# First two token blocks multiplied in plain float32: operands undivided, the norm's g moved into the weight conversion, schedule positions set anew

## The chip, the cores and the metric

The kernel runs on one core of one Trainium2 chip. The metric is device microseconds of one execution. Engines are named as in the profile: PE (TensorE matmul; PEld is its weight load), DVE (VectorE), ACT (ScalarE), POOL (GpSimd), SP (the engine whose queue issues nearly all DMAs).

## The reference, cut to what matters

Eight heads of a linear attention are normalised row by row, laid side by side as a 4608 x 512 matrix x, and sent through a two-layer network with a softplus between the layers.

```python
q, k, v: (8, 8, 576, 64) float32          # batch, heads, tokens, head_dim
w_in: (512, 2048), w_out: (2048, 512)     # come out of numpy as float64
kv  = np.einsum('bhsd,bhse->bhde', k, v)
out = np.einsum('bhsd,bhde->bhse', q, kv)
rms = np.sqrt(np.mean(out * out, axis=-1, keepdims=True) + 1e-06)
x   = (out / rms * g_norm).astype(np.float32)    # then (B,H,S,D) -> (B*S, H*D)
h   = x @ w_in
g   = np.maximum(h, 0.0) + np.log1p(np.exp(-np.abs(h)))
return (g @ w_out).astype(np.float32)
```

## The kernel before

**Divided operands.** The two large multiplications run in fp32r, a matmul form that keeps fewer bits than float32. To keep the accuracy, each operand is divided into three fp32r parts, and each product is three fp32r matmuls that accumulate in one PSUM bank. A part is made by a copy that rounds (ACT, `high`), a subtraction (DVE, `low`) and a multiply-add (DVE, `less`). Weights need one ACT operation more (`low_up`, line 514) and end with `third` (ACT). Of the first eight weight tiles the step `less` is done by two matmuls with the identity (`less_by_pe`, lines 525 and 526) in place of DVE.

**Tiles and steps.** Tokens are cut into 36 tiles of 128 and into 12 blocks of three tiles (384 tokens); d_ff = 2048 is cut into 16 chunks of 128. The first phase works on one block and one chunk per `step(s)`: four chunks for each of blocks 0 to 3 and six for each of blocks 4 to 11, 64 steps in all. A step is `mm1` (12 matmuls of 128x384, line 864), softplus on ACT (line 886), the division of its result g into three parts (ACT line 888, DVE lines 875 and 879), and `mm2` for each of the three tiles (3 matmuls of 128x512 each, line 871, so nine a step). Phases 1 and 2 do the remaining chunks on blocks of 512 tokens with a seven-product scheme (`wide_step`, products on line 1066, second layer on line 1137); partial sums go through DRAM.

**What comes ahead of a step.** For a tile of x: k and v of its batch are loaded and multiplied (`kv_of`, line 696), the result is copied by ACT (line 704), q is loaded and transposed (PE line 776, later DVE line 751), the rows are q times kv (`out_rows`, line 720), ACT squares them (line 793), DVE sums (line 724), POOL takes the root (lines 727 and 728), DVE multiplies (`norm`, line 732), and PE transposes the tile (line 738). For the six tiles of blocks 0 and 1 the transposed tile is then divided from PSUM (`split`: ACT line 640, DVE lines 643 and 646) and also copied to DRAM for the later phases (ACT line 802, SP line 803). Later tiles are loaded from DRAM again (`x_again`, line 841) and then divided.

**Weights.** A weight tile (128 x 512) arrives as float64, 512 KB (line 423). Six DVE operations (lines 438, 442, 447, 455, 460, 464) and two ACT operations (lines 434, 451) turn it into float32. The factor g_norm of the norm is put into w_in when it is divided: ACT line 501 with the scale `g_down`, DVE line 508 with `g_col`.

**Order.** All work is recorded as tasks with an engine, a guessed duration, a position `pos` and the buffers taken and given back. A planner in the kernel (`Plan.order`) sorts the tasks by position and readiness; the instructions are then issued in that fixed order, each engine in its own queue. The lists P0 to P7 are the hand-set positions. Where the planner sees PE free before the seventh step it puts in matmuls of the identity (`warm`, line 1232) that compute nothing; the profile shows 52. Buffers are rings of slots; some slots (`heirs`) come free only when an older ring's slots on the same memory are done. The chunk loads of k and v use a ring of four slots (`e`).

Of the kernel before, what the change touches and what calls it, by code (L numbers as in the profile page):

```python
# [18 lines left out]
P = 128  # L19
# [3 lines left out]
DOWN_G = 1.0 - 0.99 * 2.0 ** -13  # L23
E = 1.0 / RADIX

# [181 lines left out]
def kernel(  # L207
# [47 lines left out]
    P0 = [-45.94, -26.77, -11.8, 0.28, -29.91, -5.64, -2.86, 3.84, -103.4, -98.98, -69.3, -76.66, -68.5, -24.67, -23.22, -34.97, 8.15, -43.02, 7.47, 9.69, 7.18, 18.16, -12.1, 4.75, 1.0, 106.19, 31.3, 6.28, 7.19, 5.22]  # L255
    P4 = [-30.17, -6.08, 16.93, -33.9, -22.35, -28.91, -17.33, -7.12, -18.68, -2.69, 0.62, 2.73, -7.38, -1.86, 1.1, 1.72, 5.22, -13.65, 3.22, 0.88, 43.88, 43.95, -0.17, -0.32, 44.8, 40.82, -20.17, -6.56, 6.41, 10.03, -10.73, 0.23, 2.8, 0.42, -9.48, -5.03]
    P5 = [1.24, -5.69, -2.28, -3.57, 1.72, 0.53, 6.68, -5.83, 3.01, -2.95, 3.35, 1.4, -6.96, 0.27, -5.34, -2.29]
    P6 = [1.05, 6.24, 4.29, 4.08, -1.52, -2.85, 1.21, -0.34, 3.11, 3.1, -1.07, -0.73, -0.88, 9.99, 5.7, 5.69, 0.13, 0.46]
    P7 = [-23.78, -17.98, -11.85, -14.93, 0.41, 1.61, 7.35, 2.7, -25.02, -6.6, -15.2, -4.48, -2.14, 0.64, 2.93, 0.97, 4.67, 5.36, 3.33, 6.57, -10.37, 2.36, -14.11, -9.89, -7.11, 12.91, -2.89, 14.55, 12.59, 9.35]
    CONVERT, FETCH, EARLY, LATER = P0[:8], P0[8:16], P0[16:27], P0[27:]  # L260
    P1 = [49.11, 48.77, 51.0, 80.9, 122.61, 131.29, 2.87, 53.84, 71.21, 480.08, 304.47, 150.69]
    P2 = [24.08, 35.56, 23.68, 37.26, 50.08, 83.13, 74.26, 112.0, 102.25, 108.09, 139.38, -110.13, 88.34, 208.35, 423.47, -209.77, 170.15, -245.78, 423.49, 179.94, -7.53]
    P3 = [2.14, 2.48, 6.41, -16.53, 0.86, 2.79, 4.01, -16.44, 3.79, 3.96, 2.19, 1.79, 0.72, 1.35, 1.55, -1.03]
# [3 lines left out]
    EARLIER = P3[15]  # L267
    PACE = 2.5
    BY_PE = 12
    AT_ONCE = 2 * TB  # L270
# [11 lines left out]
    g_down = const.tile([P, 1], F32, name="g_down")  # L282
# [24 lines left out]
    pieces = sb.tile([P, 12, PIECE], F32R, name="pieces")  # L307
    for i in range(3):
# [4 lines left out]
    minus_r = space("gv1", 4 * WIDE, False, F32R)[:, 3 * NT:3 * NT + P]  # L313
# [5 lines left out]
                 h=2, o=2, tp=1, s0=1, s1=1, s2=1, s3=1, w=15, wh=3, u=4, u1=1, gvp=2, xl=2, ab=2)  # L319
# [7 lines left out]
    heirs.update({("w", 12 + i): [("n", 3 * i + j) for j in range(3)] for i in range(3)})  # L327
    plan = Plan(rings, heirs)
    slot, add = plan.slot, plan.add

    def new(s, shape, dtype=F32):
# [17 lines left out]
        elif r == "w":  # L349
            s.tile = shaped(pieces[:, i] if i < 12 else space(f"w{i}", PIECE, True, F32R), shape, dtype)  # L350
        elif r == "n":
            s.tile = shaped(space(f"w{12 + i // 3}", PIECE, False)[:, i % 3 * d_model:], shape, dtype)
        elif r == "wh":
# [46 lines left out]
    factors_done = {}  # L400
# [13 lines left out]
    def weight(j, pos, fetch_pos, behind):  # L414

        c, of_out = divmod(j, 2)
        raw, w = slot("rawb" if j % 2 and c < 8 else "raw"), slot("m")
# [9 lines left out]
        if wide:  # L427
# [30 lines left out]
            def rest():  # L458
                pf = p.tile.bitcast(F32)
                nc.vector.scalar_tensor_tensor(out=pf, in0=words_of()[0], scalar=2.0 ** -52, in1=pf,  # L460
                                               op0=ALU.mult, op1=ALU.mult)

            def total():
                nc.vector.tensor_tensor(out=new(w, [P, d_model]), in0=t.tile.bitcast(F32),
                                        in1=p.tile.bitcast(F32), op=ALU.add)
# [9 lines left out]
        else:  # L475
            ready = add("DVE", 450, lambda: nc.vector.tensor_copy(new(w, [P, d_model]), raw.tile[:, :, 0]),
                        [f], pos, [w], [raw])
        if c < OWN:
            divide(j, w, ready, pos, c < 4)
# [4 lines left out]
    def divide(j, w, ready, pos, by_pe=False):  # L484

        c, of_out = divmod(j, 2)
        dst = slot("w")
        w_slots[of_out, c] = dst
        factors_done[of_out, c] = split_weight(w, lambda x: x, d_model, dst, [ready], pos, not of_out, by_pe)

    def split_weight(w, part_of, n, dst, ready, pos, of_in, by_pe=False):

        d = slot("m")

        def src():
            return part_of(w.tile)

        def high():
            x = new(dst, [P, 3, n], F32R)[:, 0]
            if of_in:  # L500
                nc.scalar.activation(x, src(), func=AF.Identity, scale=g_down)
            else:
                nc.scalar.activation(x, src(), func=AF.Copy, scale=DOWN)

        def low():
            hi = dst.tile.bitcast(F32)[:, 0]
            if of_in:
                nc.vector.scalar_tensor_tensor(out=new(d, [P, n]), in0=src(), scalar=g_col, in1=hi,
                                               op0=ALU.mult, op1=ALU.subtract)
            else:  # L510
                nc.vector.tensor_tensor(out=new(d, [P, n]), in0=src(), in1=hi, op=ALU.subtract)

        def low_up():
            nc.scalar.activation(dst.tile[:, 1], d.tile, func=AF.Copy, scale=RADIX)

        def less():
            nc.vector.scalar_tensor_tensor(out=d.tile, in0=d.tile, scalar=-RADIX, in1=dst.tile.bitcast(F32)[:, 0],
                                           op0=ALU.mult, op1=ALU.add)

        def third():  # L520
            nc.scalar.activation(dst.tile[:, 2], d.tile, func=AF.Copy, scale=-E / (1.0 + E))

        def less_by_pe():
            y = new(bank, [P, n])
            nc.tensor.matmul(y, lhsT=ident_r, rhs=dst.tile[:, 0], start=True, stop=False)
            nc.tensor.matmul(y, lhsT=minus_r, rhs=dst.tile[:, 1], start=False, stop=True)

        def third_of_bank():
            nc.scalar.activation(dst.tile[:, 2], bank.tile, func=AF.Copy, scale=-E / (1.0 + E))

        more = 0 if n == d_model else -210
        a = add("ACT", (710 if of_in else 640) + more, high, ready, pos, [dst])
        b = add("DVE", (750 if of_in else 700) + more * 1.25, low, [a], pos, [d], [w])
        if by_pe:
            bank = slot("h")
            e = add("ACT", 640, low_up, [b], pos, [], [d])
            b2 = add("PE", 500, less_by_pe, [e], pos, [bank])
            e2 = add("ACT", 600, third_of_bank, [b2], pos, [], [bank])
            return [a, e, e2]
        e = add("ACT", 640 + more, low_up, [b], pos)  # L540
        b2 = add("DVE", 700 + more * 1.25, less, [b, e], pos)
        e2 = add("ACT", 640 + more, third, [b2], pos, [], [d])
        return [a, e, e2]

# [8 lines left out]
    def both(p, fetch, pos):  # L553
# [16 lines left out]
        def rest():  # L570
# [9 lines left out]
                         split_weight(w0, lambda x: x, d_model, forms[p][0], [l0], pos, True),  # L580
                         split_weight(sa, lambda x: x, d_model, forms[p][1], [d2], pos + 0.1, True),
                         split_weight(sb_, lambda x: x, d_model, forms[p][2], [d4], pos + 0.2, True),
                         split_weight(w1, lambda x: x[:, q4:], q4, forms[p][3], [l1], pos + 0.3, True)]
        for c in (2 * p, 2 * p + 1):
            if c >= OWN:
                w, ld = load_weight(2 * c + 1, fetch + 0.4)
                divide(2 * c + 1, w, ld, pos + 1.4)

    forms, forms_done, w_there = {}, {}, {}
# [38 lines left out]
    def split(t, x, ready, pos):  # L628
        n, i = divmod(t, TB)
        if i == 0:  # L630
            xv_slots[n] = slot("xv")
# [6 lines left out]

        def high():
            nc.scalar.activation(cols(0, F32R), x.tile, func=AF.Copy, scale=DOWN)  # L640

        def low():
            nc.vector.tensor_tensor(out=cols(1, F32R), in0=x.tile, in1=cols(0), op=ALU.subtract)  # L643

        def less():
            nc.vector.scalar_tensor_tensor(out=cols(2, F32R), in0=cols(1), scalar=-RADIX, in1=cols(0),
# [20 lines left out]
    def kv_of(b):  # L667
# [7 lines left out]
        for p in range(NP + 1):  # L675
            tail = p == NP
            ks, vs = (slot(f"tail{i}" if tail else "e") for i in range(2))
# [29 lines left out]
    def rows(t):  # L707
# [90 lines left out]
        if t < BY_PE:  # L798
            a = add("PE", 440, turn_x, [a], pos + 0.5, [xp], [x])
            if t < AT_ONCE:  # L800
                split(t, xp, a, pos + 0.5)
            a = add("ACT", 600, lambda: nc.scalar.copy(new(xg, [P, KD, P]), xp.tile), [a], pos + 1, [xg], [xp])
# [46 lines left out]
    def step(s):  # L849
        n, c = ORDER[s]  # L850
        cs = CHUNKS[n]
        h, g, gv = slot("h"), slot("g"), slot("gv")
# [4 lines left out]
        kept = c >= 4  # L857

# [15 lines left out]
        def low():  # L874
            nc.vector.tensor_tensor(out=gv.tile[:, 1], in0=g.tile, in1=gv.tile.bitcast(F32)[:, 0], op=ALU.subtract)

        def less():
            f32 = gv.tile.bitcast(F32)
            nc.vector.scalar_tensor_tensor(out=gv.tile[:, 2], in0=f32[:, 1], scalar=-RADIX, in1=f32[:, 0],
# [6 lines left out]
        a = add("ACT", 490, lambda: nc.scalar.activation(new(g, [P, NT]), h.tile, func=AF.Softplus, scale=1.0 + E),  # L886
# [13 lines left out]
    sums, mm2s = [], {}  # L900

# [11 lines left out]
    def leave(ph, t, bank, done, pos):  # L913

        ot = slot("m")
        if ph == LAST and t == n_tiles - 1:
# [15 lines left out]
            new(ot, [P, d_model]), bank.tile, func=AF.Copy, scale=scale if ph == LAST else 1.0),  # L932
# [335 lines left out]
```

## Time and profile before

Three runs took 857.61, 857.70 and 859.12 us (median 857.7). The profiled execution has a span of 856.4 us from its first to its last instruction, 1.3 us less than the median.

| engine | busy us | share | instructions |
|---|---|---|---|
| PE | 843.0 | 98% | 6464 |
| PEld | 754.1 | 88% | 6464 |
| DVE | 704.1 | 82% | 995 |
| ACT | 520.6 | 61% | 980 |
| POOL | 76.6 | 9% | 79 |

| event of the start | us from the span's start |
|---|---|
| first DVE operation on a weight (line 438) | 4.73 |
| last chunk of batch 0's k issued, landed | 12.59, 18.49 |
| first multiplication by the norm (line 732) | 25.69 |
| first `mm1` (line 864) begins | 44.09 |
| first `mm2` (line 871) begins | 58.26 |
| sixth `mm1` begins | 78.84 |

A busy PE is not always PE at work: its matmuls are shown with their whole passage, and the fillers on line 1232 count as busy. How the work stands is read from the start times in the chain of waits and in the timeline. The granted clock is full in all 40 slices of the page. The DMA engines' mean share is 1.08 between 4.0 and 26.5 us (315 GB/s) and 0.94 between 26.5 and 79 us (244 GB/s).

### The profile page before, as it was taken

Reading aid. Unit: us, or ns where it says so; the run is one execution under the profiler, and the core shown is the slowest. Engines: PE = TensorE matmul, PEld = TensorE weight load, DVE = VectorE, ACT = ScalarE, POOL = GpSimd, SP = SyncE. Lnnn points to the kernel's source line nnn. Section 1 sums busy time; section 2 is a strip of 40 time slices with the busy share of each in tenths; the row PEclk is TensorE's granted clock in tenths of the full one; section 3 lists DMA queues with packets and bytes.
Section 4 is the critical chain, followed back from the end, with each engine's and each line's share of the span. In section 5 each row is a group of like instructions: output and inputs, shape, how many; then the busy total and the mean of one; then the engine's idle time right before and its main releaser. Section 6 shows DMA issues by size and latency. Waiting matters only on the chain.

```text
span 856.4 us, 17075 instructions
## 1 busy us (share of the span) xinstructions
PE 843.0 (98%) x6464; PEld 754.1 (88%) x6464; DVE 704.1 (82%) x995; ACT 520.6 (61%) x980; POOL 76.6 (9%) x79
## 2 busy tenths in 40 slices
PE   8899999999999999999999999999999999999998
PEld 5578898999898999999999999998999899999996
DVE  7888898888788889798898788878788766788873
ACT  6766665446344567766667665655868555566654
POOL 0351223111113300000000000000000000000000
PEclk9999999999999999999999999999999999999999
DMA  9998997778884755436644546645364753777864
GB/s 283 297 233 212 261 273 232 185 245 218 214 188 119 194 160 185 142 110 207 210 156 154 180 151 206 195 158 181 124 197 138 234 168 102 240 237 246 249 189 131
DMA packets 239778, 167.07 MB, mean 195 GB/s; under 512 B 106320, under 2 KB 198736, under 8 KB 239696
## 3 DMA queue, kind: packets, MB, share of 16 engines
q1 hardware_dynamic: 239392, 165.86, 65.9%
q8 instruction: 50, 0.82, 0.4%
q14 instruction: 32, 0.26, 0.1%
q10 hardware_dynamic: 304, 0.13, 0.1%
HBM read 112.98 MB, written 52.95 MB: 194 GB/s over the span
## 4 chain that ended last, share of the span: by engine, by line
PE 94%; ACT 1%; DVE 1%; DMA 1%; issue 1%; POOL 0%; SPq 0%; POOLq 0%; DVEq 0%; ACTq 0%
PE banks L1137 31%; PE banks L1066 28%; PE banks L871 16%; PE banks L864 15%; PE banks L720 2%; PE banks L696 2%; DMA loads<-in_k_dram 1%; PE banks L738 0%; PE banks L1232 0%; PE banks L776 0%; DVE units L643 0%; DVE half L732 0%; DVE roots L724 0%; POOL roots L728 0%; ACT w L783 0%
## 5 line engine op out<-in xcount | busy, mean ns | idle before, releaser
L1137 PE MATMUL banks<-pieces,gv 128*128 128x512 f32 x768 | 236.8, 390 | 0.0
L1137 PE MATMUL banks<-pieces,g_False 128*128 128x512 f32 x384 | 149.4, 389 | 0.0
L1137 PEld LDWEIGHTS banks<-pieces,gv 128*128 128x128 f32 x768 | 132.5, 188 | 17.2 <-DVE banks L910 0.2
L864 PE MATMUL banks<-units,pieces 128*128 128x384 f32 x768 | 144.8, 337 | 0.0
L871 PE MATMUL banks<-pieces,gv 128*128 128x512 f32 x576 | 143.3, 393 | 0.0
L864 PEld LDWEIGHTS banks<-units,pieces 128*128 128x128 f32 x768 | 134.7, 188 | 4.5
L871 PEld LDWEIGHTS banks<-pieces,gv 128*128 128x128 f32 x576 | 106.2, 188 | 19.0
L1066 PEld LDWEIGHTS banks<-units,pieces 128*128 128x128 f32 x840 | 111.0, 188 | 6.5 <-ACT banks L1112 0.4
L1066 PE MATMUL banks<-units,pieces 128*128 128x256 f32 x840 | 115.2, 280 | 0.0
L886 ACT ACTIVATE half<-banks 128x384 f32<-128x384 f32 x64 | 31.4, 491 | 94.0 <-PE banks L864 90.7
L1127 DVE TENSOR_TENSOR gv<-g_True,gv 128x1024 fp32r<-128x1024 f32 x47 | 57.5, 1223 | 35.6 <-ACT gv L1124 35.5
L1137 PEld LDWEIGHTS banks<-pieces,g_False 128*128 128x128 f32 x384 | 72.1, 188 | 15.0
L1066 PEld LDWEIGHTS banks<-units,w 128*128 128x128 f32 x504 | 66.7, 188 | 3.7 <-ACT banks L1112 0.2
L1066 PE MATMUL banks<-units,w 128*128 128x256 f32 x504 | 69.6, 280 | 0.0
L728 POOL TENSOR_TENSOR roots<-roots,half 128x8 f32<-128x8 f32 x36 | 62.3, 1731 | 3.0
L1130 DVE SCALAR_TENSOR_TENSOR g_False<-gv 128x1024 fp32r<-128x1024 f32 x47 | 57.6, 1225 | 1.5
L1029 DVE TENSOR_TENSOR units<-loads,units 128x1024 fp32r<-128x1024 f32 x42 | 51.2, 1219 | 6.0 <-ACT units L1026 5.9
L1094 ACT ACTIVATE g_True<-banks 128x256 f32<-128x256 f32 x96 | 36.7, 384 | 30.6 <-PE banks L1066 29.9
L1116 DVE TENSOR_TENSOR g_True<-banks,g_True 128x512 f32<-128x512 f32 x48 | 33.1, 690 | 25.8 <-PE banks L1066 19.8
L931 ACT ACTIVATE m<-banks 128x512 f32<-128x512 f32 x72 | 42.1, 595 | 18.2 <-PE banks L1137 12.5
L1032 DVE SCALAR_TENSOR_TENSOR units<-units 128x1024 fp32r<-128x1024 f32 x42 | 51.4, 1224 | 1.7
L1026 ACT ACTIVATE units<-loads 128x1024 fp32r<-128x1024 f32 x42 | 44.3, 1056 | 12.4 <-PE banks L1066 10.1
(115 smaller groups left out, 1248.7 us busy)
## 6 DMA issues: line engine op xcount, KB each, us to landing
loads<-x SPq DMA_DIRECT2D x180, 128.0 KB, 2.7
part<-m SPq DMA_DIRECT2D x72, 256.0 KB, 3.1
m<-part SPq DMA_DIRECT2D x72, 256.0 KB, 3.4
loads<-form SPq DMA_DIRECT2D x45, 256.0 KB, 3.2
form<-loads SPq DMA_DIRECT2D x36, 256.0 KB, 3.0
raw<-in_moe_w_in_dram SPq DMA_DIRECT2D x16, 512.0 KB, 4.7
loads<-in_k_dram SPq DMA_DIRECT2D x32, 256.0 KB, 4.0
loads<-in_v_dram SPq DMA_DIRECT2D x32, 256.0 KB, 4.5
```

The costliest lines, as they stand in the source:

```text
L728: nc.gpsimd.tensor_tensor(out=r.tile, in0=r.tile, in1=half, op=ALU.pow)
L864: nc.tensor.matmul(from_the_end(hp, w), lhsT=w_in.tile[:, i, kd * P:(kd + 1) * P], rhs=from_the_end(xv.tile[:, i, kd], w), start=(m == 0), ...
L871: nc.tensor.matmul(mine[i].tile, lhsT=gv.tile[:, m, i * P:(i + 1) * P], rhs=w_out.tile[:, m], start=(c == cs[0] and m == 0), stop=(c == cs ...
L931: a = add("ACT", 690 if ph == LAST else 600, lambda: nc.scalar.activation(new(ot, [P, d_model]), bank.tile, func=AF.Copy, scale=scale if p ...
L1026: nc.scalar.activation(part_of(0, F32R), xl.tile if m > 1 else xl.tile[:, 0], func=AF.Copy, scale=DOWN)
L1029: nc.vector.tensor_tensor(out=part_of(1, F32R), in0=xl.tile if m > 1 else xl.tile[:, 0], in1=part_of(0), op=ALU.subtract)
L1032: nc.vector.scalar_tensor_tensor(out=part_of(2, F32R), in0=part_of(1), scalar=-RADIX, in1=part_of(0), op0=ALU.mult, op1=ALU.add)
L1066: nc.tensor.matmul(from_the_end(place(q), (16, 8)[kd]), lhsT=w[:, m, at:at + P], rhs=from_the_end(dst.tile[:, m, v, kd] if u < 6 else dst. ...
L1094: nc.scalar.activation(dst, src, func=AF.Softplus, scale=1.0 + E)
L1127: nc.vector.tensor_tensor(out=gvt(1, F32R), in0=gt(), in1=gvt(0), op=ALU.subtract)
L1130: nc.vector.scalar_tensor_tensor(out=gt(F32R), in0=gvt(1), scalar=-RADIX, in1=gvt(0), op0=ALU.mult, op1=ALU.add)
L1137: nc.tensor.matmul(from_the_end(mine[i].tile, P), lhsT=(gvt(m, F32R) if m < 2 else gt(F32R))[:, c, i * P:(i + 1) * P], rhs=from_the_end(ou ...
```

## The change

The first two blocks (`PLAIN = 2`), that is the first eight steps, are multiplied in plain float32. For them x is stored undivided in the ring `xf` (one ACT copy, from which the DRAM store is also made), the result of softplus is used undivided, and the weights are used as they come out of the conversion (ring `f`). A step is then 4 matmuls of 128x384 and one matmul of 128x512 for each tile; in the first two steps `mm1` is issued tile by tile, 4 matmuls of 128x128 for each (`BY_TILES`). Later blocks still take the divided weights of chunks 0 to 3, so these are divided all the same, at positions of their own (`DIVIDE`). Rings `f` and `xf` lie on the memory of five of the twelve `pieces` slots, which come free when the plain blocks are done.

The norm's g is multiplied into w_in in the last two conversion steps (`rest` with `g_low`, `total` with `g_col`), so that all weights are divided alike, with one ACT operation less (`low_up` falls away). The eight weights whose `less` was done on PE now do it on DVE (`BANKED = False`). Signs and scales are moved between the parts. The chunk loads of k and v for batch 0 use four more slots (ring `m`). All positions are new numbers.

```diff
-    P0 = [-45.94, -26.77, -11.8, 0.28, -29.91, -5.64, -2.86, 3.84, -103.4, -98.98, -69.3, -76.66, -68.5, ...
+    P0 = [-31.3, -30.64, -54.26, -2.58, -36.38, -151.12, -27.16, 4.44, -244.63, -199.65, -214.44, -165.6, ...
...
+    DIVIDE, BANKED, STORE, AFTER = P8, False, 1.0, 1.5
+    BY_TILES, CHAIN = 2, False
+    PLAIN = 2
-    AT_ONCE = 2 * TB
+    AT_ONCE = PLAIN * TB
...
-    pieces = sb.tile([P, 12, PIECE], F32R, name="pieces")
+    pieces = sb.tile([P, 7, PIECE], F32R, name="pieces")
+    for i in range(7, 12):
+        space(f"w{i}", PIECE, False)
...
+    heirs.update({("w", 8 + i): [("f", j) for j in range(3 * i, min(3 * i + 3, 8))] for i in range(3)})
+    heirs.update({("w", 7): [("xf", 0)], ("w", 11): [("xf", 1)]})
...
-        raw, w = slot("rawb" if j % 2 and c < 8 else "raw"), slot("m")
+        raw, w = slot("rawb" if j % 2 and c < 8 else "raw"), slot("f" if c < 4 else "m")
...
-                nc.vector.scalar_tensor_tensor(out=pf, in0=words_of()[0], scalar=2.0 ** -52, in1=pf,
+                nc.vector.scalar_tensor_tensor(out=pf, in0=words_of()[0], scalar=2.0 ** -52 if of_out else g_low, in1=pf,
                                                op0=ALU.mult, op1=ALU.mult)
...
+                if of_out:
+                    nc.vector.tensor_tensor(out=y, in0=tf, in1=pf, op=ALU.add)
+                else:
+                    nc.vector.scalar_tensor_tensor(out=y, in0=tf, scalar=g_col, in1=pf, op0=ALU.mult, op1=ALU.add)
...
-            divide(j, w, ready, pos, c < 4)
+            if c < 4:
+                plain[of_out, c] = w, [ready]
+                pos = DIVIDE[j]
+            divide(j, w, ready, pos, c < 4 and BANKED)
...
-        a = add("ACT", (710 if of_in else 640) + more, high, ready, pos, [dst])
-        b = add("DVE", (750 if of_in else 700) + more * 1.25, low, [a], pos, [d], [w])
+        a = add("ACT", 640 + more, high, ready, pos, [dst], follows=taken[-1] if taken and chain else None)
+        b = add("DVE", 700 + more * 1.25, low, [a], pos, [], [w])
...
-        e = add("ACT", 640 + more, low_up, [b], pos)
-        b2 = add("DVE", 700 + more * 1.25, less, [b, e], pos)
-        e2 = add("ACT", 640 + more, third, [b2], pos, [], [d])
+        b2 = add("DVE", 700 + more * 1.25, both_of, [b], pos, [d])
+        return [b, add("ACT", 640 + more, third, [b2], pos, [], [d])]
...
+        if n < PLAIN:
...
+            a = add("ACT", 600, whole, [ready] + ([] if i == 0 else [first_high[n]]), pos, [dst] if i == 0 else [], [x])
...
+            x_there[t] = [add("SP", 450, store, [a], pos + STORE, [], [dst], 1000)]
+            return
...
-            ks, vs = (slot(f"tail{i}" if tail else "e") for i in range(2))
+            ks, vs = (slot(f"tail{i}" if tail else "m" if not b and p > 1 else "e") for i in range(2))
...
+    def plain_step(s, n, c, cs, h, g, xv, mine):
+        (w_in, in_done), (w_out, out_done) = plain[0, c], plain[1, c]
+        def mm1(i0=0, n=TB):
+            hp = (h.tile if i0 else new(h, [P, NT]))[:, i0 * P:(i0 + n) * P]
+            for kd in range(KD):
+                nc.tensor.matmul(hp, lhsT=w_in.tile[:, kd * P:(kd + 1) * P], rhs=xv.tile[:, kd, i0 * P:(i0 + n) * P],
+                                 start=(kd == 0), stop=(kd == KD - 1))
+        def mm2(i):
+            if c == cs[0]:
+                new(mine[i], [P, d_model])
+            nc.tensor.matmul(mine[i].tile, lhsT=g.tile[:, i * P:(i + 1) * P], rhs=w_out.tile,
+                             start=(c == cs[0]), stop=(c == cs[-1]))
...
```

172 lines of the change are left out of this document (98 added, 74 removed).

## The prediction

> **What bounds the kernel now.** I read the page's chain that ended last first: it lies almost wholly on PE.
>
> ```profile
> PE 94%; ACT 1%; DVE 1%; DMA 1%; issue 1%; POOL 0%; SPq 0%; POOLq 0%; DVEq 0%; ACTq 0%
> ```
>
> The same chain in order of time tells where the other six per cent are (start, duration, what):
>
> ```profile
> 12.59 5.90 DMA loads<-in_k_dram
> 18.62 1.15 PE banks L696 x32
> ...
> 21.04 1.14 PE banks L720 x64
> 22.20 0.61 ACT half L793
> 22.83 1.28 DVE roots L724 x2
> ...
> 44.25 2.09 PE banks L864 x12
> ...
> 78.45 0.64 PE banks L738 x4
> 79.09 2.11 PE banks L864 x12
> 81.20 0.44 PE banks L738 x4
> 81.64 2.09 PE banks L871 x9
> 83.73 2.09 PE banks L864 x12
> 85.82 2.04 PE banks L871 x9
> ```
>
> Up to 78.8 us the chain runs from engine to engine; behind that one PE piece follows the other to 852.6 us, and the view of PE's waits lists none after 79 us. Two windows say it with sums (PE, PEld, DVE, ACT, POOL busy, clock, DMA share, GB/s):
>
> ```profile
> 26.50:79.00 52.50, 47.93 (x680) 38.68 (x681) 45.94 (x79) 36.03 (x72) 20.20 (x19) 1.00 0.94 244
> 79.00:319.00 240.00, 240.00 (x2215) 216.12 (x2215) 206.67 (x354) 128.28 (x252) 52.65 (x50) 1.00 0.78 208
> ```
>
> In the first PE has fillers and 5 `mm1`, while DVE works 46 of 52.5 us: the start is bound by what DVE prepares. So the time is (moment from which PE never waits) + (PE work left), and the change must be judged by both.
>
> **The yardstick.** At 78.84 us before has done 5 `mm1` and 4 steps of `mm2`. In the order of the built new kernel, the first fp32r `mm1` (block 2) stands behind all eight plain steps, as many attention pieces as before had at 78.84 us, and one x transpose more. Before would reach that content after 3 x 2.09 + 4 x 2.04 + 0.41 = 14.8 us more, at 93.7 us. Behind it both kernels hold the same fp32r `mm1`, `mm2` and wide products. If the new kernel reaches it at T and stays dense, the gain is 93.7 - T.
>
> **Price of a plain matmul.** No row shows it at 128x384 or 128x512; its count and duration come from other float32 rows.
>
> ```profile
> L864 PE MATMUL banks<-units,pieces 128*128 128x384 f32 x768 | 144.8, 337 | 0.0
> L871 PE MATMUL banks<-pieces,gv 128*128 128x512 f32 x576 | 143.3, 393 | 0.0
> ...
> L1066 PE MATMUL banks<-units,pieces 128*128 128x256 f32 x840 | 115.2, 280 | 0.0
> ...
> L720 PE MATMUL banks<-early,w 64*64 64x64 f32 x1152 | 22.0, 222 | 1.2 <-ACT half L793 0.6 <-ACT w L802 0.4
> L696 PE MATMUL banks<-loads 128*64 128x64 f32 x512 | 19.3, 226 | 2.0 <-DMA loads<-in_v_dram 1.1 <-DMA loads<-in_k_dram 0.7 <-DVE units L643 0.2
> ...
> L738 PE MATMUL banks<-ident_r,half 128*128 128x128 f32 x48 | 7.5, 280 | 0.9 <-ACT pieces L514 0.5 <-DVE half L732 0.4
> ```
>
> L720 and L696 multiply plain float32: 576 and 320 (512 + 128 with the tails) matmuls in the order, twice as many records here, so a matmul is two records. The fp32r rows lie near 170 + 0.43 ns per column (280, 337, 393 at 256, 384, 512), which gives 197 ns at 64 columns; the float32 records take 222 to 226, about one more stream of 64 columns. So I take two streams a record, four a matmul. In the chain an fp32r record takes 174 ns at 384 columns and 227 at 512: 0.414 ns a column and 15 ns fixed. A plain record is then 2 x 384 x 0.414 + 15 = 333 ns, or 439 at 512, or 121 at 128. A plain `mm1` is 8 x 333 = 2.66 us against 2.09, tile by tile 24 x 121 = 2.9; `mm2` of a step is 6 x 439 = 2.63 against 2.04. Low end: one stream a record, 1.39 and 1.36. High end: L696 passes 32 records of 64 columns in 1.08 us, 0.53 ns a column, and if its two halves of the array run side by side one alone takes 1.06: 3.26 and 3.24. I take the middle, the only one that fits the durations.
>
> The Trainium skill, FP8 and Floating Point Precision, section TensorE Precision Notes, has true FP32 as four passes through the array. By it the sum is the middle one, and three fp32r products become four passes; the trace's durations agree, its spacing of L696 alone would allow less.
>
> Eight plain steps: 2 x 2.9 + 6 x 2.66 + 8 x 2.63 = 42.8 us, where fp32r took 8 x 4.13 = 33.0. PE pays 9.8 us; the 16 identity matmuls of lines 525 and 526 go, about 0.5 us a pair, in time that was idle.
>
> **What the preparation loses.** DVE: 12 divisions of x (12 x 0.69 = 8.2 us) and 16 of g (16 x 0.556 = 8.9) go; 8 `less` come back from PE (+5.5); the scalar columns in `rest` and `total` add 0.06 to each of 32 (+1.9, lines 508 against 517: 746 and 683 ns); `low` of 29 w_in divisions loses as much (-1.8): 11.5 us net, nearly all before T. ACT: 45 `low_up` (26.5 us), 6 copies and 8 high parts of g go (7.8 us), off the path (ACT is 61% busy); without that cover they would sit between DVE's steps.
>
> **When the first plain step begins.** The new SP order puts batch 0's k and v ahead of the weights. Its last chunk has 4224 KB at or before it in the queue against 4864 KB; before, it landed at 18.49 us, 3.4 us per 1000 KB after about 2 us, so now 16.3. The attention rows move by 2.2 us: sums at 20.6, first `norm` near 23.4, second near 25.6 (POOL's 2.1 us each). The price is the first weight, 2048 KB into the queue and not 512: DVE starts on it near 9.5 us, not 4.73, and w_out 0 and w_in 1 at 15 and 18 us, ahead of the sums. Then transposes (0.4), an ACT copy (0.6), and `mm1` of tile 0, which stands behind the transpose of tile 1, at 26.5; no division of x nor of a weight is waited for. Before: 44.09.
>
> **The sum.** PE from there to T: plain steps 42.8, and attention pieces standing in between by their spacings, 13 groups of transposes at 0.40 (5.2), eight groups of kv products at 0.54 and two of tails at 0.57 (5.5), eight of rows times kv at 0.62 (5.0): 15.7. T = 26.5 + 58.5 = 85.0 if PE never waits. DVE to the third divided tile of block 2: its instructions in the new order at their spacings in the timeline (0.46 to 0.68 us) make 69.2 us, against 68.9 before to its own, which ended at 81.6 with 8.0 us of waits; so 9.5 + 69.2 + 8.0 = 86.7. For PE I add half of its waits between 26.5 and 79 us before (4.7): 85.0 + 2.3 = 87.3. Both queues agree; T = 87.2, gain 6.5. Span 856.4 - 6.5 = 849.9; with the 1.3 us between span and median, **851.2**. One wait is added: the divisions of chunk 4's two weights go into memory that comes free with the last plain `mm1`. Two ACT copies wait there, and behind them on ACT the softplus of that very step and the copy of block 2's third tile; on DVE ten instructions (5.5 us) up to that tile's division. On PE 1.7 us of attention and two `mm2` (5.3 us) stand between that `mm1` and T, 7.0 us, which covers them; without that cover it would be 5.5 us. SP keeps its 812 rows; the six x stores only come from another tile. The new positions of the later phases I cost at nothing, since PE's dense stream hides the order of the others; without cover every late preparation is paid in full.
>
> **Rivals.**
> (a) *DVE takes PE's place in the fp32r steps.* Up to the g of step 20 the new order has 126.5 us of DVE work against 134.9, 8.4 less, but begins 4.8 later: 3.6 us ahead where PE wants 6.5. For it: DVE is 86% busy there. Against: its 33 us of idle in 79 to 319. If nothing absorbs it, the gain is 3.6: 854.1.
> (b) *Plain records stream once.* PE's start work is 18 us less, and DVE with half its waits ends at 9.5 + 69.2 + 4.0 = 82.7: gain 11.0, 846.7. Against: the 222 to 226 ns.
> (c) *Slower: a plain matmul costs the high end,* because nothing runs beside it. Place: the eight plain steps, 52.0 us and not 42.8; T = 96.4, 2.7 us behind: 860.4. It decides from 15% above my price (1.01 us for a plain 128x512). For it: no plain matmul of full width is in the trace.
> That the change does nothing is excluded: the built order holds 48 + 24 matmuls from undivided tiles and 96 + 72 fewer fp32r ones.
>
> **How the numbers follow.** Forecast 0.45 (its own range 848.5 to 852.8), (a) 0.22, (b) 0.12, (c) 0.21. The range 846.0 to 859.0 takes in the first three and the near part of (c). A measurement tells 0.2% (1.7 us) from no change: faster, under 856.0, is 0.45 + 0.12 + 0.19 of (a) = 0.76; within, 0.03 of (a) and 0.05 of (c) = 0.08; slower 0.16.
>
> **What would show it.** Two records of 128x512 per plain `mm2`, 0.44 us apart; first plain `mm1` at 25 to 28 us; the first fp32r `mm1` at 85 to 90; no PE wait of size behind it; DVE near 692 us and ACT near 486 busy. I am wrong if the first plain matmul waits for a weight's landing, if records stand more than 0.5 us apart, or if waits on DVE appear on PE behind T.

## The result, and the profile after

| | runs | median us | range |
|---|---|---|---|
| before | 4 | 858.3 | 857.6 to 859.1 |
| after | 4 | 863.9 | 862.9 to 864.5 |

The ratio is 1.0063, with a 95% interval of 1.0049 to 1.0078: the changed kernel is 5.6 us slower. Its profiled execution has a span of 861.8 us, 5.4 more than before. The forecast was 851.2.

The first thing to read is what the forecast had priced with most care. These are the groups of the new kernel's first phase (line, engine, operation, tiles and shapes, count, busy us, mean ns, idle before):

```profile
L889 PE MATMUL banks<-units,pieces 128*128 128x384 f32 x480 | 91.3, 338 | 0.0
L896 PE MATMUL banks<-pieces,gv 128*128 128x512 f32 x270 | 67.0, 392 | 0.0
...
L940 PE MATMUL banks<-w,half 128*128 128x512 f32 x48 | 23.1, 603 | 0.0
...
L934 PE MATMUL banks<-w,w 128*128 128x384 f32 x48 | 16.6, 488 | 0.0
```

The fp32r rows are as before. The plain rows hold two records for each matmul (24 matmuls each, 48 records). Their spacing is read from the chain of waits in the new kernel (start, duration, what):

```profile
81.86 2.58 PE banks L934 x8
86.14 5.35 PE banks L940 x12
91.49 2.11 PE banks L889 x12
```

Twelve plain records of 512 columns take 5.35 us, 0.446 each where 0.439 was forecast; eight of 384 columns take 2.58 us where 2.66 was forecast. The Trainium skill's four passes for true FP32 (FP8 and Floating Point Precision, TensorE Precision Notes) agree with both.

Engine shares of the chain that ended last and the two windows shown of before (PE, PEld, DVE, ACT, POOL busy, clock, DMA share, GB/s):

```profile
PE 93%; DMA 4%; ACT 1%; DVE 1%; SPq 1%; POOL 0%; issue 0%; ACTq 0%; DVEq 0%
```

```profile
26.50:79.00 52.50, 50.41 (x592) 33.83 (x593) 45.04 (x75) 34.43 (x70) 21.82 (x19) 1.00 0.95 261
79.00:319.00 240.00, 239.10 (x2234) 209.70 (x2233) 205.29 (x352) 122.45 (x241) 51.32 (x50) 1.00 0.78 210
```

In the second window PE now has 0.9 us of idle where it had none, which is not 5 us. DMA has 4% of the chain where it had 1%: 33 us in the chain's pieces against 10.7, and 26.9 of the 33 lie ahead of 73 us, in the start, which is taken up below. The price was right, these windows look alike, and the kernel is slower all the same. To see where, one figure is used in all that follows: take a moment t and add, for each matmul record that starts later, its spacing in dense work (174 and 227 ns for the fp32r records of lines 889 and 896, 117 for a wide product, 227 for wide `mm2`, 34, 19.4 and 105 for kv, rows and x transposes). That is the **end if PE were dense from t on**. Where it grows with t, PE loses time.

| end if dense from t = | 100 us | 140 | 340 | 840 |
|---|---|---|---|---|
| before | 850.7 | 851.3 | 852.5 | 852.7 |
| after | 848.3 | 851.0 | 851.9 | 857.9 |

At 100 us the new kernel is 2.4 us ahead. By 140 us 2.1 of them are gone. From 340 us on, in the wide phases, it loses 6.0 us where before lost 0.2. In the wide phases' own tasks the diff changes position numbers, signs and scales, and no work.

The waits of PE's weight loads from 340 to 860 us name the place, first in the new kernel and then in the one before (what <- what it waited for: us in all, times, longest):

```profile
PEld banks L1127 <- ACT banks L1173: 5.9, 25, 0.6
PEld banks L1127 <- ACT g_True L1152: 0.4, 2, 0.2
PEld banks L1127 <- ACT banks L1169: 0.2, 1, 0.2
```

```profile
PEld banks L1066 <- ACT banks L1112: 0.6, 3, 0.2
PEld banks L1137 <- DVE banks L910: 0.2, 1, 0.2
```

Line 1173 (1112 before) is the copy `Z <- Y`. In each wide step one product (`a6`) writes Y, ACT copies Y to Z, and two products (`a3`, `a7`) go on from the copies. One such place in PE's timeline of the new kernel (start, duration, ..., idle before):

```profile
560.32 0.86 PE L1127 MATMUL banks<-units,w 128*128 128x256 f32 x6
561.02 0.62 PE L1198 MATMUL banks<-pieces,gv 128*128 128x512 f32 x2
561.48 0.39 PE L1198 MATMUL banks<-pieces,g_False 128*128 128x512 f32 x1
561.70 1.69 PE L1127 MATMUL banks<-units,w 128*128 128x256 f32 x12
```

and ACT's and the weight loads' rows beside it:

```profile
561.28 0.36 ACT L1173 COPY banks<-banks 128x256 f32<-128x256 f32 x1 [2.18 <-PE banks L1127]
```

```profile
561.25 0.19 PEld L1198 LDWEIGHTS banks<-pieces,g_False 128*128 128x128 f32 x1
561.68 1.50 PEld L1127 LDWEIGHTS banks<-units,w 128*128 128x128 f32 x12 [0.24 <-ACT banks L1173]
```

The product's last results are there at 561.18, the copy runs from 561.28 to 561.64, the next weights are loaded at 561.68. From the start of `a6` to its successor's first load that is 1.36 us, and PE has one `mm2` group (0.68 us) to put between. PE itself shows no idle, since its rows are shown with their whole passage; the loss is in the 12 records that take 1.69 us there against 1.56 where the loads run ahead, and in a few hundredths on each group until they do so again. In the orders as built, `a6` and `a3` have exactly one `mm2` group between them 24 times in the 48 wide steps of the new kernel, 3 times before; three groups stand there 5 and 16 times.

### The profile page after: what moved, and what is told of

Read it like the earlier page. It is cut to its first block, busy times and chain, and to the rows that moved or that the text cites. A ratio compares the mean times of both kernels' runs of the same rounds, so it can differ in the third digit from the quotient of the medians.

```text
span 861.8 us, 16844 instructions
## 1 busy us (share of the span) xinstructions
PE 849.1 (99%) x6405; PEld 742.5 (86%) x6405; DVE 694.4 (81%) x974; ACT 489.5 (57%) x921; POOL 76.5 (9%) x79
## 4 chain that ended last, share of the span: by engine, by line
PE 93%; DMA 4%; ACT 1%; DVE 1%; SPq 1%; POOL 0%; issue 0%; ACTq 0%; DVEq 0%
PE banks L1198 30%; PE banks L1127 28%; PE banks L889 14%; PE banks L896 14%; PE banks L741 2%; PE banks L717 2%; PE banks L934 2%; PE banks L940 2%; DMA g<-in_moe_w_out_dram 1%; DMA m<-w_spill 1%; DMA raw<-in_moe_w_in_dram 1%; DMA loads<-in_v_dram 1%; DMA part<-m 1%; PE banks L759 0%; POOL roots L749 0%
## 5 line engine op out<-in xcount | busy, mean ns | idle before, releaser
L1198 PE MATMUL banks<-w,gv 128*128 128x512 f32 x408 | 126.4, 391 | 0.0
L1198 PE MATMUL banks<-pieces,gv 128*128 128x512 f32 x360 | 111.7, 391 | 0.0
L1188 DVE TENSOR_TENSOR gv<-gv,g_True 128x1024 fp32r<-128x1024 f32 x47 | 57.5, 1223 | 46.1 <-ACT gv L1185 46.1
L889 PE MATMUL banks<-units,pieces 128*128 128x384 f32 x480 | 91.3, 338 | 0.0
L889 PEld LDWEIGHTS banks<-units,pieces 128*128 128x128 f32 x480 | 84.2, 188 | 3.3 <-issue 0.5
L1127 PEld LDWEIGHTS banks<-units,pieces 128*128 128x128 f32 x600 | 78.6, 188 | 4.3 <-ACT banks L1173 0.7
L1198 PE MATMUL banks<-w,g_False 128*128 128x512 f32 x204 | 79.3, 389 | 0.0
L1198 PEld LDWEIGHTS banks<-w,gv 128*128 128x128 f32 x408 | 70.5, 188 | 9.4
L1198 PE MATMUL banks<-pieces,g_False 128*128 128x512 f32 x180 | 70.1, 390 | 0.0
L1198 PEld LDWEIGHTS banks<-pieces,gv 128*128 128x128 f32 x360 | 61.5, 188 | 7.5
L896 PE MATMUL banks<-pieces,gv 128*128 128x512 f32 x270 | 67.0, 392 | 0.0
L1090 DVE TENSOR_TENSOR units<-units,loads 128x1024 fp32r<-128x1024 f32 x42 | 51.3, 1221 | 11.3 <-ACT units L1087 10.9
L896 PE MATMUL banks<-w,gv 128*128 128x512 f32 x234 | 58.8, 393 | 0.2 <-DVE gv L904 0.2
L896 PEld LDWEIGHTS banks<-pieces,gv 128*128 128x128 f32 x270 | 50.0, 188 | 8.7
```

The lines of the kernel that those rows point to most:

```text
L889: nc.tensor.matmul(from_the_end(hp, w), lhsT=w_in.tile[:, i, kd * P:(kd + 1) * P], rhs=from_the_end(xv.tile[:, i, kd], w), start=(m == 0), ...
L896: nc.tensor.matmul(mine[i].tile, lhsT=gv.tile[:, m, i * P:(i + 1) * P], rhs=w_out.tile[:, m], start=(c == cs[0] and m == 0), stop=(c == cs ...
L1090: nc.vector.tensor_tensor(out=part_of(1, F32R), in0=part_of(0), in1=xl.tile if m > 1 else xl.tile[:, 0], op=ALU.subtract)
L1127: nc.tensor.matmul(from_the_end(place(q), (16, 8)[kd]), lhsT=w[:, m, at:at + P], rhs=from_the_end(dst.tile[:, m, v, kd] if u < 6 else dst. ...
L1188: nc.vector.tensor_tensor(out=gvt(1, F32R), in0=gvt(0), in1=gt(), op=ALU.subtract)
L1198: nc.tensor.matmul(from_the_end(mine[i].tile, P), lhsT=(gvt(m, F32R) if m < 2 else gt(F32R))[:, c, i * P:(i + 1) * P], rhs=from_the_end(ou ...
```

## The experiments

Each was timed in five rounds beside the kernel before (its median 858.4 to 858.8 in these sessions). "End" is the end if dense at the two moments.

| run | median us | ratio to before, 95% interval | end from 340 | from 840 | waits on the copy |
|---|---|---|---|---|---|
| e1_late_old | 872.8 | 1.0174 (1.0155 to 1.0192) | 865.1 | 867.3 | 1.4 us, 7 times |
| e2_weights_new | 860.1 | 1.0011 (1.0002 to 1.0020) | 851.7 | 853.7 | 1.5, 7 |
| e3_old_with_new_wide | 872.1 | 1.0168 (1.0154 to 1.0182) | 852.3 | 865.9 | 3.9, 11 |
| e4_copy_twice | 875.0 | 1.0194 (1.0180 to 1.0208) | 852.6 | 867.8 | 15.8, 27 |
| e5_product_earlier | 858.9 | 1.0000 (0.9992 to 1.0009) | 851.8 | 852.8 | 0.2, 1 |
| e6_weights_new_earlier | 858.3 | 0.9994 (0.9985 to 1.0003) | 853.3 | 854.4 | 0.5, 1 |
| e7_weight_first | 864.6 | 1.0065 (1.0052 to 1.0077) | 852.8 | 858.8 | 5.4, 24 |
| e8_earlier_mm1_swap | 859.8 | 1.0012 (1.0001 to 1.0023) | 851.7 | 852.8 | 0.5, 1 |
| e9_attention_first | 866.5 | 1.0090 (1.0069 to 1.0110) | 857.3 | 858.4 | 0.5, 1 |
| e10_weight9_later | 860.0 | 1.0016 (1.0001 to 1.0030) | 853.1 | 854.2 | 0.5, 1 |
| e11_attention_first_2 | 863.4 | 1.0051 (1.0037 to 1.0065) | 856.1 | 857.1 | 0.5, 1 |
| e12_mask_of_8 | 859.0 | 1.0001 (0.9992 to 1.0011) | 852.9 | 853.7 | 0.5, 1 |

### The wide phases

**e1_late_old.**

```diff
-    P1 = [57.49, 48.45, 65.67, ...
+    P1 = [49.11, 48.77, 51.0, ...
...
-    P6 = [1.5, 9.94, 2.49, -38.82, -78.8, ...
+    P6 = [1.05, 6.24, 4.29, 4.08, -1.52, ...
```

P2 and P3 likewise.

> The new kernel with four lists of positions of the old one: those of the wide phases and of the work that prepares them (P1, P2, P3, P6); start, plain steps and fp32r steps stay new. Theory A (the loss arises in the wide phases: the new order leaves only one group of mm2 between the product that ACT's copy Z<-Y waits for and the product that waits for that copy, 23 times against 4, and PE stalls or runs slower for some 5.5 us between 400 and 750 us): 863.9 - 5.5 = 858.4, within 857.0 to 859.8, idle before PEld's products behind that copy under 2 us and not 5.2. Rival B (the loss comes from the plain blocks and from what they do to memory and DVE, whatever the later order): 862.5 or more. First fp32r mm1 near 91 us by both.

Measured: 872.8, worse than anything expected. From 340 us on it loses 2.2 us and not 6.0, with 1.4 us of waits on the copy, as theory A has it. But 13.7 us are lost between 140 and 340. The waits of PE from 190 to 345 us in this run show part of it:

```profile
PE banks L1127 <- ACT early L1087: 4.2, 1, 4.2
PE banks L741 <- DVE half L753: 1.3, 1, 1.3
```

The old positions of the later preparations do not fit the new first phase: the first wide product stands for its divided x. Lists tuned together can't be exchanged in part without a new loss.

**e2_weights_new** keeps the new P2 and takes only P1, P3 and P6 from the kernel before (edit as above).

> The new kernel with the old P1, P3 and P6; of the later lists only P2 (when the weights of chunks 6 to 15 are taken and divided) stays new. In its built order the place with one mm2 group before the product that waits for the copy is there 8 times, the one with three groups 21 times (new kernel 23 and 6, old kernel 4 and 16). Theory A: as without the loss, 858.5 (857.0 to 860.0). Rival B: 862.5 or more. Rival C (the loss lies in the new positions of the weights, P2, whose conversions come late): 861 to 864, with waits on DVE at PE's products.

Measured: 860.1, 0.1 above theory A's range, and 2.0 us lost from 340 us on. Some 3.8 us of the loss come back with the plain blocks, their memory and the weights' positions all as in the new kernel. Rivals B and C fall for that share.

**e3_old_with_new_wide.**

```diff
-    P3 = [2.14, 2.48, 6.41, ...
+    P3 = [1.03, 0.05, 7.95, ...
...
-    P6 = [1.05, 6.24, 4.29, 4.08, -1.52, ...
+    P6 = [1.5, 9.94, 2.49, -38.82, -78.8, ...
```

> The kernel before with the new P3 and P6 (positions within a wide step and of the x units). Its order has the one-group place 13 times, the three-group place 6 times (4 and 16 before). Theory A: slower than before by some 2 to 5 us, 860.3 to 863.3. Rival B: 858.3 within 1 us, since nothing of the plain blocks is in it.

Measured: 872.1, slower by 13.3 us and so far outside theory A's 2 to 5. Only 3.9 us of its waits are on the copy; others are on line 1091 (4.3 us) and line 1108 (2.0), two other copies that ACT makes in a wide step. It shows that positions alone can cost more than 10 us in the wide phases of the old kernel too, and nothing on the size of the copy's share.

**e4_copy_twice.**

```diff
-        c6 = add("ACT", 380, lambda: nc.scalar.copy(place(Z), place(Y)), [a6], b + 0.65)
+        c6 = add("ACT", 380, lambda: (nc.scalar.copy(place(Z), place(Y)), nc.scalar.copy(place(Z), place(Y)))[1], [a6], b + 0.65)
```

> The new kernel with the copy Z<-Y done twice on ACT (the second writes the same values), order unchanged. One copy takes 0.36 us. Theory A: where one mm2 group or fewer stands between, PE waits for it, some 25 to 30 of 56 steps: 25 x 0.36 = 9.0 us more, 873 (869 to 878). Rival B: this copy is not on PE's path but where a chain needs an end, at most 2 us more, 864 to 866.

Measured: 875.0, 11.1 us more than the new kernel. The waits behind the copy go from 5.9 us in 25 places to

```profile
PEld banks L1127 <- ACT banks L1173: 15.8, 27, 0.6
```

9.9 us more, 0.37 for each of 27 places: one copy. (The wide steps are 48, not 56.) The copy is on PE's path there and rival B falls.

**e5_product_earlier** changes PE's order of issue alone: after the planner, `a6` is moved ahead of up to two of the `mm2` groups before it where fewer than three follow.

```diff
+    for t in [t for t in pe if getattr(t, "kind2", None) == "frees"]:
+        ...
+        if j < i and getattr(pe[i + 1 + between], "kind2", None) == "needs":
+            ts.remove(t)
+            ts.insert(ts.index(pe[j]), t)
```

> The new kernel, all positions new; only the order of issue on PE in the wide phases is mended by hand: where fewer than three mm2 groups stand between the product that ACT's copy Z<-Y waits for and the product that needs the copy, the first product is moved ahead of up to two of the mm2 groups before it (one group between: 24 places before, 1 now). The copy was done twice in another run and cost 11 us more, so it is on PE's path. Theory A (that spacing is the wide phases' loss): 863.9 - 4.5 = 859.4 (858 to 861), idle of PE's weight loads behind the copy under 2 us in all. Rival C (the spacing is only a sign of later preparations being late, which then become the wait): 862.5 or more, with waits on DVE or on another copy in its place.

Measured: 858.9, 5.0 us less than the new kernel, and from 340 us on 1.0 us lost and not 6.0. The same place in its timeline:

```profile
556.14 0.86 PE L1127 MATMUL banks<-units,w 128*128 128x256 f32 x6
556.84 0.62 PE L1200 MATMUL banks<-pieces,gv 128*128 128x512 f32 x2
557.29 0.39 PE L1200 MATMUL banks<-pieces,g_False 128*128 128x512 f32 x1
557.52 0.62 PE L1200 MATMUL banks<-pieces,gv 128*128 128x512 f32 x2
557.97 0.39 PE L1200 MATMUL banks<-pieces,g_False 128*128 128x512 f32 x1
558.20 1.56 PE L1127 MATMUL banks<-units,w 128*128 128x256 f32 x12
```

Two groups stand between, the copy (557.09 to 557.45) ends 0.75 us before the product that needs it, and 12 records take 1.56 us. Nothing else was moved, and no other wait came in its place. This is the cause of the wide phases' loss, shown by itself.

**e6_weights_new_earlier** puts e2's lists and e5's mending together.

> The kernel of e2 (new kernel, old P1, P3, P6) with the same mending: one group between at 1 place or fewer and not at 7. Theory A: the 1.9 us that e2 still loses from 340 us on against dense work fall to 0.7: 860.1 - 1.2 = 858.9 (858.0 to 859.8). Rival C: 860 or more.

Measured: 858.3, level with the kernel before. Its start happened to be 1.3 us later than e5's in the profiled execution (end from 100 us: 849.4 and 848.1), though the order there is the same; the start scatters by about that much.

### The start

**e7_weight_first.**

```diff
+    first = [t for t in ts if t.engine == "SP"][7]
+    ts.remove(first)
+    ts.insert(0, first)
```

> The new kernel with one DMA moved in SP's queue: the first weight ahead of batch 0's k and v (place 1 and not 8), everything else in the new order. Theory D (the start is set by the attention chain, k's last chunk, sums, POOL's roots; DVE's late begin costs nothing): first DVE work on a weight near 5 us and not 10.64, k's last chunk still near 19.5, first plain mm1 30.0 within 0.7, first fp32r mm1 91 within 0.7; 863.9 within 1.0. Rival E (DVE's work that began 5.5 us late is what makes PE wait for DVE between 100 and 140 us, 2 us): first fp32r mm1 no earlier, but that wait gone: 861.5 to 862.5.

Measured: 864.6, as the new kernel. DVE begins on a weight at 5.75 us and not 10.64, and then stands:

```profile
17.32 0.69 DVE L520 SCALAR_TENSOR_TENSOR pieces<-pieces,w 128x512 fp32r<-128x512 f32 x1 [7.49 <-ACT pieces L517]
```

In order of issue, DVE had nothing to do but to wait for later landings. The first plain `mm1` begins at 31.2 us, later than theory D allowed (30.0 within 0.7), and the first fp32r `mm1` comes at 92.3 us in the chain (91.5). The loss from 100 to 140 us is still there, so rival E falls. Theory D holds in the main: 4.9 us at DVE's begin were worth nothing.

**e9_attention_first** and **e11_attention_first_2** move tasks of the first 30 us in the built list (both on e6). e11's core:

```diff
+    move([k_3], of["loadq_0"])
+    move(["kv0.3", "kv0.4", "kvcopy_0"], of["turnq_0"])
+    move(["rows_0", "square_0"], behind(copies[0]))
+    ...
+    move(["norm_0", "turnx_0", "whole_0", "rows_2", "square_2", "mm1_0.0"], conv[1][4])
```

> The kernel of e6 with the start put in another order of issue: batch 0's last k chunk goes ahead of the q pieces in SP's queue; the last kv products, the rows of tiles 0 and 1, their sums and roots go ahead of the work on w_out 0 in each queue, the norm and transposes of tiles 0 and 1 and the first two mm1 pieces ahead of w_in 1's and of batch 1's; the fillers behind the first mm1 are left out. It asks whether the step of the forecast that failed at the start (k's last chunk at 16.3 us, first mm1 at 26.5) is only a matter of order. Theory H (DVE's first sums stood behind the work on weights that land at 17.4 and 21.1 us, so landing k earlier was not enough): k's last chunk near 15, sums near 18.5 to 19 and not 23.0, first plain mm1 at 26.4 (25.4 to 27.4) and not 29.95, first fp32r mm1 1 to 3.5 us earlier than 90.9, time 855 to 857.5. Rival I (the DMA queues are the bound of the start, the bytes that come earlier push the rest back): first plain mm1 later than 28, time within 0.8 of e6.

Measured: 866.5. The kv products of k's last chunk began at 17.5 us (19.5), the first sum at 21.0 (23.0), but the first plain `mm1` at 31.9: the norms had been put behind work that still waited. Theory H's 26.4 was not reached; rival I has the late `mm1` right and the time wrong. While PE waited 4.3 us for the first norm its clock fell (last section), so this run settles nothing on its own. The fillers that were left out are not the reason: they stand behind the first `mm1`, and the clock fell 7.9 us ahead of it.

> The kernel of e6 with the start in a second order of issue, fillers kept: k's last chunk ahead of the q pieces in SP's queue; on PE its kv products ahead of the transposes of q, the rows of each tile right behind that tile's q; sums of tiles 0 and 1 before and within the work on w_out 0, their norms before its last step and before w_in 1's work, tile 2's norm behind that. Theory H (the start is set by the order in which the queues serve the first tiles): first sum near 16.5 us and not 23.0, first norm near 20 and not 26.1, first plain mm1 at 22 to 24 us and not 29.95, first fp32r mm1 at 87.5 to 90 and not 90.9, time 855 to 857.5. Rival L (DVE's conversions and divisions, some 69 us of work behind the first weight at 10.64 us, bound the plain steps whatever the attention does first): first plain mm1 that early, but first fp32r mm1 within 1 us of 90.9 and time within 1 us of 858.3.

Measured: 863.4. Here the early part went as theory H had it: first sum at 17.0, first norm at 22.1, first plain `mm1` at 24.2 us, 5.7 us earlier than in the new kernel. And yet, in the chain of this run (its line 908 is the fp32r `mm1`):

```profile
90.11 5.35 PE banks L960 x12
95.46 2.11 PE banks L908 x12
```

the first fp32r `mm1` came 4.0 us later than in the new kernel, and the time is 5.1 us above e6's. Neither theory's numbers came out, and the moment of the first plain `mm1` alone does not set that of the first fp32r one.

**e12_mask_of_8.**

```diff
-                tf = t.tile.bitcast(F32)
-                nc.vector.scalar_tensor_tensor(out=tf, in0=sq.tile, scalar=2.0 ** 64, in1=tf,
+                tf = t.tile.bitcast(F32)[:, :8]
+                nc.vector.scalar_tensor_tensor(out=tf, in0=sq.tile[:, :8], scalar=2.0 ** 64, in1=tf,
```

> The kernel of e6 with one DVE operation of every weight conversion, the mask of line 458 that clears the smallest values, done on 8 of its 512 columns: the masking of the other columns is left out. Order and dependences stay. Ten of them (0.69 us each, 0.6 in the spacing) stand before the first fp32r mm1, so DVE has 6 us less to do there. Theory M (DVE sets the moment of the first fp32r mm1: in the new kernel its third divided tile of block 2 ends at 91.1 us = begin at 10.64 + 69.6 of work + 10.9 of waits, and mm1 follows at once; and it is the bound from 100 to 122 us again): first fp32r mm1 2 to 4 us earlier, at 87 to 89.5, the loss from 100 to 140 us under 1.5 and not 2.8; time 854 to 856.5. Rival N (PE's own queue or the landings set it, and DVE's idle only grows): first fp32r mm1 within 1 us of 91, time 857.5 or more.

Measured: 859.0, and the first fp32r `mm1` at 92.6, as in the profile of e6 (92.6). Each of the ten operations took 0.17 us and not 0.69, some 5.2 us less, and DVE's waits took all of it: those for w_in's landings alone are 11.2 us (8.4 in the new kernel). Theory M falls. DVE's amount of work does not set that moment either.

Two readings are left. The first is the DMA engines' time. Windows of the new kernel and of e11 (PE, PEld, DVE, ACT, POOL busy, clock, DMA share, GB/s):

```profile
10.00:20.00 10.00, 8.23 (x75) 5.64 (x73) 7.55 (x13) 5.87 (x12) 0.00 (x0) 1.00 1.01 289
20.00:30.00 10.00, 8.45 (x206) 6.61 (x202) 8.86 (x15) 6.38 (x15) 4.02 (x4) 1.00 1.03 291
30.00:40.00 10.00, 9.72 (x170) 8.83 (x168) 9.09 (x16) 6.72 (x15) 5.08 (x4) 1.00 0.94 252
```

```profile
10.00:20.00 10.00, 8.63 (x141) 6.68 (x140) 6.65 (x12) 5.24 (x11) 2.16 (x2) 1.00 1.07 288
20.00:30.00 10.00, 7.84 (x71) 5.96 (x71) 6.65 (x13) 5.22 (x11) 4.82 (x5) 0.83 0.71 203
30.00:40.00 10.00, 8.42 (x133) 7.01 (x134) 7.59 (x13) 6.05 (x14) 1.02 (x2) 1.00 0.79 229
```

The share (1 is all 16 engines) times 10 us gives 29.8 us for the new kernel, 25.7 for e11 and 24.9 for e9 from 10 to 40 us: 4.1 and 4.9 less. Their first fp32r `mm1` came 4.0 and 5.6 us later (95.46 and 97.12 against 91.49). In e7 (30.5) and e12 (29.8) no share was lost, and it came within 1.2 us. By this reading the transfers bound the start, and an order that leaves them idle pays for it. Against e6, from which e9 and e11 were made (29.6, and 92.59), the match is looser: 3.9 and 4.7 us of share, 2.9 and 4.5 us of delay. And the runs e2 and e5, with the new kernel's order at the start, have 29.3 and 31.2 us of share and reach the first fp32r `mm1` at 91.32 and 91.37.

The second reading is that e11's own order held DVE up, and that the idle transfers only follow from it. DVE's largest waits in e11 from 10 to 92 us, behind that for the first weight, are on ACT (what <- what it waited for: us in all, times, longest):

```profile
DVE roots L756 <- ACT half L828: 5.1, 5, 2.9
DVE m L459 <- ACT sq L446: 2.6, 4, 1.3
DVE half L764 <- ACT half L828: 1.6, 1, 1.6
```

From 12 to 92 us DVE waits 11.3 us for ACT (4.4 in the new kernel), and 0.6 for landings (2.0). The chain of e11 has no transfer between 4.6 and 71.3 us. For e11 this speaks for the second reading. Neither was tried by itself, with fewer bytes to move or with ACT's order alone put right, and what sets the first fp32r `mm1` in the new kernel stays open.

### From 100 to 140 us

**e8_earlier_mm1_swap.**

```diff
+    ts.remove(of["mm1_13"])
+    ts.insert(ts.index(of["rows_16"]), of["mm1_13"])
```

> The kernel of e6 with one exchange on PE at 117 us: the mm1 of step 13, whose operands are ready, goes ahead of the attention rows of tile 16, which wait for DVE's norm to free a bank (0.6 us on PE, 0.9 us at its weight load). Theory F (PE stands there only because of the order): 0.6 to 0.9 us less than e6, some 858.1. Rival G (DVE is the bound from 108 to 122 us, 94% busy, and the wait comes back at the next mm2): within 0.3 us of e6.

**e10_weight9_later** moves a conversion: `conv` behind `less_13`, its division behind `less_14`.

> The kernel of e6 with the conversion of w_out 4 (six DVE operations, 3.4 us, first needed at step 20) moved on DVE and ACT behind the division of step 13's g, and its own division behind that of step 14. Theory J (the 2 us lost between 100 and 140 us are DVE's: it is 94% busy from 110 to 120 us with attention rows, the divisions of g and this conversion): PE's wait for the rows at 117 us and the late mm2 of step 12 shrink by 0.8 to 1.3 us, time 857.1 (856.6 to 857.7). Rival K (the work only moves, and PE waits at the mm2 of step 14 for it): within 0.4 of e6's 858.3.

Measured: 859.8 and 860.0, neither faster than e6's 858.3. In e8 the rows' wait of 0.6 us became one of 1.5, in e10 one of 0.9 at an `mm1` for a divided tile of x appeared. Theories F and J fall. The rivals are not confirmed either: G and K allowed 0.3 and 0.4 us from e6, and these runs lie 1.5 and 1.7 above it.

The 2.1 us lost there stay without a cause that was shown. PE's own waits in the new kernel are 0.8 us, but its weight loads wait 3.0 us there for other engines and landings, and in the kernel before for none of them:

```profile
PEld banks L741 <- ACT half L911: 0.9, 1, 0.9
PEld banks L896 <- DVE gv L904: 0.5, 1, 0.5
PEld banks L896 <- DVE gv L900: 0.4, 1, 0.4
```

The other three, of 0.4 each, are on ACT, DVE and a landing of q. Also, 59 more records stand in that stretch (507 and 448), mostly attention, whose switches the figure does not price.

## Why the prediction was wrong

**Two steps failed.** The forecast was 12.7 us too low, and the count above divides it: 5.8 in the wide phases, 4.3 at the start, 2.1 from 100 to 140 us, and 0.8 because the profiled execution is 2.1 us below the median and not 1.3. The sum is 13.0.

*"The new positions of the later phases I cost at nothing, since PE's dense stream hides the order of the others."* This decided the sign. PE was dense in the profile of before because its order had room around nearly every copy. The new numbers leave ACT's copy one `mm2` group in 24 of 48 steps. This can be counted in the built order, and the prediction did not count it. e4 shows that the copy is on the path at those places, e5 that the spacing costs 5.0 us. With it mended, the changed kernel is level with the one before (e5 1.0000, e6 0.9994) and not 6.5 us ahead.

*"T = 87.2, gain 6.5."* Of the terms, the plain steps were right. The first plain `mm1` began at 29.95 us and not 26.5, and the time from there was 61.5 us where 60.8 was forecast, so T was 91.5 and the gain on the yardstick's 93.7 only 2.2. The 26.5 came from a landing of k's last chunk at 16.3 us by "3.4 us per 1000 KB"; it landed at 19.35. Two things differed from before. The pieces ahead of it were smaller ones: from 4 to 14 us the new kernel moved 2.94 MB in 6165 packets at a share of 1.10, before 3.17 MB in 5315 at 1.09. And from 14 us to the landing the share was 0.88 (273 GB/s), where before had 1.09 (346 GB/s); why it fell is not shown. A price by KB did not hold between the two orders.

```profile
DMA packets 6165, 2.94 MB, mean 294 GB/s; under 512 B 4313, under 2 KB 6159, under 8 KB 6165
```

But a first `mm1` at 26.5 need not have made T 87.2 either: in e11 it came at 24.2 and T was 95.5. The sum took DVE's and PE's queues as the two that could set T. An earlier begin of DVE's work (e7), less of it (e12) and an earlier first `mm1` (e11) did not bring T forward, and what does is open.

**Rivals.** (a) had DVE take part of the gain in the fp32r steps, 2.9 us; 2.1 were lost there, with 1.3 us of waits for DVE at PE's weight loads, and that DVE does it is not shown. (b) and (c) are out by the plain records' 0.322 and 0.446 us. The slower outcome came by a mechanism that the prediction did not list. "No PE wait of size behind it" came out true for PE's own rows from 340 us on, and the loss was there all the same: the waits stood in PE's weight loads, on ACT. "Waits on DVE ... on PE behind T" came to 0.2 us.

**What was right.** Busy times after are 694.4 us for DVE (692 forecast) and 489.5 for ACT (486). SP kept its rows. The wait for memory behind the last plain `mm1` cost nothing that the trace shows.

## What to carry to other kernels

When positions of a whole schedule are new, read the built order of the phases that the change does not mention: for each short operation between two dependent matmuls count what PE has to put between, and compare it with the time from the first matmul's start to the next weight load (here 1.36 us, of which the copy is 0.36). A start in which the DMA engines' share is 1.0 for tens of microseconds should be priced by its transfers too, by packets as well as by bytes, and not by two engines' queues alone; that the transfers bound this one was not shown. A loss of this kind is mended in the order alone: moving one product in some 25 places gave back 5.0 us.

## What was not expected of the hardware

The clock that the profile shows for PE fell in runs whose start left PE idle. In e9, which had no fillers there, PE stood from 21.8 to 26.1 us; windows of 1 us (PE, PEld, DVE, ACT, POOL busy, clock, DMA share, GB/s):

```profile
23.00:24.00 1.00, 0.00 (x0) 0.00 (x0) 0.90 (x2) 0.00 (x0) 0.92 (x2) 0.99 0.61 149
24.00:25.00 1.00, 0.00 (x0) 0.00 (x0) 0.93 (x3) 0.79 (x2) 0.92 (x2) 0.50 0.10 21
```

It came back near 30.8 us, and the first x transposes (line 770) took 424 ns each in between and 280 ns later. In e6 it fell to 0.50 near 25.5 us after a wait of only 2.4 us, and stayed there to 29 us. In e11, too, it fell near 24.5 us, where the longest wait of PE in the 3.4 us before was 1.4. The Trainium skill, TensorE: Matmul & The Clock Gate, Part 1, has the clock halve after an idle window of some 3.4 us. Here a stretch of that length that was idle only in part was enough.

A weight load that waits 0.24 us leaves no idle on PE in the profile. In the new kernel such waits were 5.9 us in all, and the order without them was 5.0 us faster.
